# Block 0 in two halves around block 1, with raw weight words loaded into their own slots

## The chip, the cores and the metric

The kernel runs on one core of one Trainium2 chip. The metric is the device time in microseconds (us); what is quoted is the median over runs. One profiled execution gives the trace that is read here.

## The reference, cut to what matters

Attention over keys and values that are averaged by eights, then two feed-forward layers on the same 4608 tokens. All inputs are of 32 or 64 bits; the two `w` of the first layer and of the second come as 64-bit words and are decoded on the chip.

```python
# q, k, v: (8 batches, 8 heads, 576, 64); pool = 8
k_p = k.reshape(B, H, Sp, pool, D).mean(axis=3)       # v_p likewise
attn = softmax(q @ k_p^T / sqrt(D))
x = (attn @ v_p)            # -> 4608 tokens x 512

h = x @ w_in                # 512 -> 2048
y = (h * cos(h)) @ w_out    # 2048 -> 512

h2 = y @ w2_in              # 512 -> 1024
solu = h2 * softmax(h2);  ln = layernorm(solu) * g_ln
out = ln @ w2_out           # 1024 -> 512
```

## The kernel before, in words

**Blocks and steps.** The tokens are cut into 9 blocks of 512 (`j`), the 2048 columns of the first layer into 16 pieces of 128 (`f`). One step is one pair (j, f); the main loop (L828) runs through 144 of them, `steps`, block by block. A step on TensorE is `h_mm` (L519, 12 matmuls into one of two PSUM buffers `h`) and, two steps late (`SK` = 2), `y_mm` (L557, 12 matmuls that add into `y`). Between the two stands a chain of small operations on 128x512 values: `t = int(h / 2pi + 1/4)` (L527, here called k, on VectorE), `t = h - 2pi t` (L532, VectorE), a sine (L536, ScalarE), `t = t * h` (L541, VectorE, one step later; it is the last reader of that `h` buffer), the rounded half of g (L543, ScalarE) and the rest of g (L547, VectorE). The matmul of step n+2 needs the `h` buffer that L541 of step n gives back.

**Decoding.** `w_in` and `w_out` are 32 chunks of 512 KB in raw words. A chunk is loaded by SyncE into a `raw` tile and goes through `Pipe`: one call of `step` moves three chunks on by one stage. Stage s1 is two operations on ScalarE (L94, L95), s2 three on VectorE (L100, L105, L110) and one addition on GpSimd (L113), s3 one copy on ScalarE (L122) and one subtraction on GpSimd (L125), into a tile `wi` or `wo`. Five calls come ahead of the main loop, and in block 0 two in every step, threaded between the operations of the chain, until all 32 chunks are done.

**Attention.** Block j+1's attention runs inside the steps of block j, from a table of half steps (`slots`, L456): scores, exponential, `norm` (L395 to L406: sums on VectorE, products `em` and `el` on GpSimd), transposes (L416, L431) with copies by ScalarE and VectorE, products with v (`av`, L448 to L454) that end in tiles `x`. Sums over eight keys or values run on GpSimd (L194, L214).

**Order.** Each engine's instructions stand in the order in which the code calls them (`manual_schedule`); an engine that waits holds up all that is behind it in its own queue. Tiles that share a tag share that pool's buffers, and a new tile waits until the old one is no longer read. The tag `s2` has four buffers, which serve the intermediate values `dec` of the decoding and the copies `yo` by which `y_out` (L562) takes a finished block out of PSUM to DRAM (`yd`). Block 8 decodes the second layer's weights with a second `Pipe` (L837), after which 36 tiles of 128 tokens run through that layer.

Of the kernel before, what the change touches and what calls it, by code (L numbers as in the profile page):

```python
# [34 lines left out]
def fused_kernel(ctx, tc, qT_d, kT_d, vN_d, vM_d, vL_d, w_in, w_out, w2_in, w2_out, g_ln, out):  # L35
# [23 lines left out]
    wp = ctx.enter_context(tc.tile_pool(name="wp", bufs=NF))  # L59
    xp = ctx.enter_context(tc.tile_pool(name="xp", bufs=2 * NPAIR))  # L60
# [4 lines left out]
    dram = ctx.enter_context(tc.tile_pool(name="dram", bufs=NB, space=bass.MemoryType.DRAM))  # L65
# [4 lines left out]
    w_in_w, w_out_w, w2_in_w, w2_out_w = (w.bitcast(I32) for w in (w_in, w_out, w2_in, w2_out))  # L70

# [11 lines left out]
    class Chunk:  # L83
        def __init__(self, kept, tag, src, g=None, pool=wp):
            self.kept, self.tag, self.src, self.g, self.pool = kept, tag, src, g, pool
# [11 lines left out]
        def s2(self):  # L97
# [6 lines left out]
            yield  # L104
# [4 lines left out]
            yield  # L109
# [5 lines left out]
        def s3(self):  # L115
            dst = self.pool.tile([P, 2, BLK], F32R, tag=self.tag, name=self.tag)
# [11 lines left out]
    class Pipe:  # L128
# [6 lines left out]
        def fill(self, most=8):  # L135

            held = [c.raw for c in self.loaded + self.one]
            while self.todo and len(held) < most:
                c, raw = self.todo[0]
                if any(raw is r for r in held):  # L140
                    break
# [5 lines left out]
        def step(self):  # L147
            for _ in self.parts():
                pass

        def parts(self):

            last = self.two.pop(0) if self.two else None
            if self.one:
                c = self.one.pop(0)
                yield from c.s2()
                self.two.append(c)
# [26 lines left out]
    def kv_jobs(b, hf):  # L184


        def raw_tile(n):
            if (b, hf) < (1, 1):
                return wp.tile([P, n], F32, tag="wi", name="kvraw")
# [7 lines left out]
        def k_job(i):  # L197
# [5 lines left out]
            def add():  # L203
                if b == 0:
                    t = wp.tile([P, SP], F32, tag="wo", name="kp")
# [31 lines left out]
    def load_vn(b):  # L237
        t = v_t[b] = [wp.tile([P, 2, BLK], F32, tag="wi", name="vn") for _ in range(3)]
# [18 lines left out]
    def prep_vn(b, hf):  # L257
# [3 lines left out]
        w = wp.tile([P, 4 * D], F32, tag="wo", name="vw")  # L261
        u = wp.tile([P, 2, 4 * D], F32, tag="wo", name="vu")
        hi = wp.tile([P, 4 * D], F32R, tag="wo", name="vh")
# [48 lines left out]
    class Attn:  # L312
# [3 lines left out]
        def __init__(self, j):  # L316
            self.j = j
            self.t0 = j * BLK
            self.x = [None] * NPAIR
            self.sm, self.qT, self.e, self.em, self.el, self.eL, self.eT = ({} for _ in range(7))  # L320
            self.sg = list(segs(self.t0, BLK))

        def tile(self, shape, dt, tag, bufs=1):
            if self.j == 0:
                return wp.tile(shape, dt, tag="wo", name=tag)
# [114 lines left out]
        def av(self, p):  # L440
# [11 lines left out]
            x = self.x[p] = xp.tile([P, 2, BLK], F32R, tag="x", name="x")  # L452
# [513 lines left out]
```

## Time and profile before

| | before |
|---|---|
| median of 3 runs | 1416.4 us (1416.36 to 1416.98) |
| profiled execution | 1415.08 us |
| its span, first to last instruction | 1413.3 us |
| TensorE busy | 1355.3 us, 96% |
| VectorE busy | 982.1 us, 69% |
| ScalarE busy | 533.1 us, 38% |
| GpSimd busy | 404.2 us, 29% |
| mean granted TensorE clock | 0.985 |

The profiled execution is 1.8 us longer than its span and 1.3 us shorter than the median. The shares are means over stages that have different limits: a short stage ahead of the main loop, block 0 with the decoding, the blocks 1 to 7, block 8 with the second decoding, and the second layer. They have to be read stage by stage. A group of rows below names its view; "mean ns of one" is the duration of a single instruction, and for instructions that follow each other on one engine the distance from start to start is some 0.08 us shorter than the duration.

### The profile page before, as it was taken

What the parts mean: (1) busy time and instruction counts of PE and PEld (TensorE: products, weight loads), DVE (VectorE), ACT (ScalarE), POOL (GpSimd) and SP (SyncE); (2) the same over time, 40 slices, a digit from 0 to 9 for tenths busy, and PEclk for the clock granted to TensorE, in tenths of its full rate; (3) what the DMA queues carried; (4) which work ended last, traced back from release to release, by engine and by line L of the source; (5) the groups of instructions that cost most, each with busy time, mean ns of one, the idle gap of its engine ahead of it and who ended that gap; (6) DMA issues with size and microseconds to landing.
All of it is one profiled execution on the core that took longest, in us unless ns stands there. A gap on an engine that the chain in (4) does not pass through costs nothing.

```text
span 1413.3 us, 17197 instructions
## 1 busy us (share of the span) xinstructions
PE 1355.3 (96%) x6304; PEld 1116.3 (79%) x6304; DVE 982.1 (69%) x1690; ACT 533.1 (38%) x891; POOL 404.2 (29%) x517
## 2 busy tenths in 40 slices
PE   6778799999999999999999999899899999999998
PEld 5566688888888888888888888688788888888887
DVE  8999966666676666666666655897666666666664
ACT  5665633333343343333333333554222222222222
POOL 3787833322332241242131101453111111111110
PEclk9999999999999999999999999999999999999999
DMA  7424111111120220220120101430111111111100
GB/s 266 149 84 143 61 61 54 40 53 46 47 69 24 61 64 15 76 63 24 52 62 9 45 1 60 118 120 23 52 50 41 48 43 47 43 48 42 46 29 31
DMA packets 43236, 85.27 MB, mean 60 GB/s; under 512 B 4112, under 2 KB 13328, under 8 KB 43152
## 3 DMA queue, kind: packets, MB, share of 16 engines
q1 hardware_dynamic: 37824, 74.72, 16.8%
q10 hardware_dynamic: 5328, 9.44, 1.8%
q8 instruction: 50, 0.82, 0.3%
q14 instruction: 34, 0.28, 0.1%
HBM read 65.28 MB, written 18.87 MB: 60 GB/s over the span
## 4 chain that ended last, share of the span: by engine, by line
PE 82%; DVE 12%; POOL 2%; issue 2%; DMA 1%; ACT 1%; SPq 0%; POOLq 0%; ACTq 0%; DVEq 0%
PE y L557 23%; PE h L519 22%; PE o L689 5%; PE o L691 5%; PE o L690 5%; PE h L619 5%; PE h L618 5%; PE h L617 5%; PE sc L351 2%; PE lT L670 2%; DVE dec L110 2%; DVE dec L105 2%; DVE dec L100 2%; DMA kvraw<-in_kT 1%; DVE t L532 1%
## 5 line engine op out<-in xcount | busy, mean ns | idle before, releaser
L519 PE MATMUL h<-x,wi 128*128 128x512 f32 x1728 | 427.0, 397 | 22.0 <-DVE t L541 22.0
L557 PE MATMUL y<-g,wo 128*128 128x512 f32 x1728 | 425.3, 395 | 6.2 <-DVE g L547 4.5
L519 PEld LDWEIGHTS h<-x,wi 128*128 128x128 f32 x1728 | 327.1, 191 | 93.4 <-DVE t L541 26.0
L557 PEld LDWEIGHTS y<-g,wo 128*128 128x128 f32 x1728 | 322.0, 189 | 74.4 <-DVE g L547 6.7
L527 DVE TENSOR_SCALAR t<-h 128x512 int32<-128x512 f32 x144 | 99.1, 688 | 148.3 <-PE h L519 148.2
L536 ACT ACTIVATE t<-t,cst 128x512 f32<-128x512 f32 x144 | 104.3, 725 | 227.5 <-DVE t L532 223.0
L543 ACT CAST g<-t 128x512 fp32r<-128x512 f32 x144 | 89.1, 619 | 197.1 <-DVE t L541 191.1
L401 POOL TENSOR_TENSOR em<-e,sm 128x512 f32<-128x512 f32 x34 | 39.6, 1166 | 333.8 <-PE y L557 324.6
L657 POOL TENSOR_TENSOR sc<-sc,cst 128x1 f32<-128x1 f32 x36 | 19.8, 551 | 367.3 <-DVE sc L656 197.5
L194 POOL TENSOR_TENSOR kvraw<-kvraw 128x256 f32<-128x256 f32 (+3 forms) x128 | 86.7, 677 | 129.4 <-DMA kvraw<-in_vM 69.4
L689 PE MATMUL o<-wi,lh 128*128 128x512 f32 x288 | 116.0, 403 | 0.0
L691 PE MATMUL o<-wi,ll 128*128 128x512 f32 x288 | 113.0, 392 | 0.0
L690 PE MATMUL o<-wi,lh 128*128 128x512 f32 x288 | 113.0, 392 | 0.0
L547 DVE TENSOR_TENSOR g<-t,g 128x512 fp32r<-128x512 f32 x144 | 109.0, 757 | 1.8 <-ACT g L543 1.8
L672 ACT CAST lh<-lT 128x512 fp32r<-128x512 f32 x72 | 38.8, 590 | 189.3 <-PE lT L670 189.3
L626 DVE TENSOR_REDUCE sc<-h 128x1 f32<-128x1024 f32 x34 | 41.6, 1225 | 91.3 <-PE h L619 91.3
L532 DVE SCALAR_TENSOR_TENSOR t<-t,h 128x512 f32<-128x512 int32 x144 | 98.8, 686 | 4.4
L541 DVE TENSOR_TENSOR t<-t,h 128x512 f32<-128x512 f32 x144 | 97.2, 675 | 5.3 <-ACT t L536 5.0
L113 POOL TENSOR_TENSOR dec<-dec,raw 128x512 int32<-128x512 int32 x48 | 69.6, 1450 | 108.3 <-DVE dec L110 43.9
L619 PE MATMUL h<-wi,yl 128*128 128x512 f32 x216 | 84.2, 390 | 0.0
L618 PE MATMUL h<-wi,yh 128*128 128x512 f32 x216 | 84.0, 389 | 0.0
L617 PE MATMUL h<-wi,yh 128*128 128x512 f32 x216 | 84.0, 389 | 0.0
(139 smaller groups left out, 1908.8 us busy)
## 6 DMA issues: line engine op xcount, KB each, us to landing
raw<-in_w_in SPq DMA_DIRECT2D x24, 512.0 KB, 3.6
raw<-in_w_out SPq DMA_DIRECT2D x24, 512.0 KB, 3.5
kvraw<-in_kT SPq DMA_DIRECT2D x32, 288.0 KB, 2.9
qT<-in_qT SPq DMA_DIRECT2D x36, 256.0 KB, 3.3
yd<-yo ACTq DMA_DIRECT2D x36, 256.0 KB, 2.5
yr<-yd SPq DMA_DIRECT2D x18, 512.0 KB, 3.8
out<-o SPq DMA_DIRECT2D x36, 256.0 KB, 2.0
kvraw<-in_vM SPq DMA_DIRECT2D x24, 256.0 KB, 2.7
```

Of the source, the lines that this page charges most:

```text
L519: nc.tensor.matmul(ps, lhsT=w[:, a, kk, :], rhs=x[kk][:, b], start=(kk == 0 and i == 0), stop=(kk == KD - 1 and i == 2),)
L527: nc.vector.tensor_scalar(out=t.bitcast(I32), in0=ps, scalar1=1.0 / TWO_PI, scalar2=0.25, op0=ALU.mult, op1=ALU.add,)
L532: nc.vector.scalar_tensor_tensor(out=t, in0=t.bitcast(I32), scalar=-TWO_PI, in1=ps, op0=ALU.mult, op1=ALU.add)
L536: nc.scalar.activation(out=t, in_=t, func=AF.Sin, bias=halfpi)
L547: nc.vector.tensor_tensor(out=g[:, 1], in0=t, in1=g[:, 0].bitcast(F32), op=ALU.subtract)
L557: nc.tensor.matmul(o, lhsT=w[:, a, P * e:P * (e + 1)], rhs=g[:, b], start=(f == 0 and i == 0), stop=(f == NF - 1 and i == 2),)
L617: nc.tensor.matmul(ps[hh], lhsT=hi[:, kk, c], rhs=w[:, 0], start=first, stop=False)
L618: nc.tensor.matmul(ps[hh], lhsT=hi[:, kk, c], rhs=w[:, 1], start=False, stop=False)
L619: nc.tensor.matmul(ps[hh], lhsT=lo[:, kk, c], rhs=w[:, 0], start=False, stop=last)
L689: nc.tensor.matmul(ps, lhsT=hi[:, c], rhs=w[:, 0], start=(c == 0), stop=False)
L690: nc.tensor.matmul(ps, lhsT=hi[:, c], rhs=w[:, 1], start=False, stop=False)
L691: nc.tensor.matmul(ps, lhsT=lo[:, c], rhs=w[:, 0], start=False, stop=(c == NF2 - 1))
```

## The change

**Order of the steps.** The list of steps is turned: steps (0, 0) to (0, 7) first, then (1, 0) to (1, 15), then (0, 8) to (0, 15), then block 2 and the others as before. Below, step n is the n-th of the list, in either kernel. The sum `y` of block 0 is written out twice, after (0, 7) and after (0, 15), into two DRAM tiles, and GpSimd adds the two when the second layer loads them (`split_y`); the second layer takes the tokens of block 1 ahead of those of block 0 (`turn`).

**Pace of the decoding.** `Pipe.step` is no longer cut into parts. While the pipe has work, a step calls it once, and a second time in the odd ones of steps 0 to 7 and in every fourth one from step 8 on. The order of the chunks follows the order in which the steps need them.

**k on ScalarE.** While the pipe has work, k runs on ScalarE (`chain_k` with `AF.Copy`), else on VectorE as before.

**Attention.** Block 1's attention has to be ready at step 8, so its table of 32 half steps is squeezed to 14, in steps 0 to 6. Block 2's is drawn over steps 12 to 31. The sums over keys of batch 1 come ahead of the main loop, those of batch 2 in steps 8 and 9.

**Slots.** Each of the 32 weight tiles has a buffer of its own (`Slots`), and from the sixth chunk on raw words mostly are loaded into the buffer that the decoded chunk will take. Tiles `x` get two fixed sets of four buffers.

```diff
+    class Slots:
+        def __init__(self, tag, n):
+            self.tag, self.n, self.next = tag, n, 0
+        def tile(self, shape, dt, name, i=None):
+            if i is None:
+                i, self.next = self.next, (self.next + 1) % self.n
+            return wp.tile(shape, dt, tag=f"{self.tag}{i}", name=name)
+    wi, wo = Slots("wi", NF), Slots("wo", NF)
...
         def load(self, raw):
-            self.raw = raw
-            nc.sync.dma_start(out=raw.rearrange("p f w -> p (f w)"), in_=self.src)
+            self.raw = raw if raw is not None else self.home([P, BLK, 2], I32, "raw")
+            nc.sync.dma_start(out=self.raw.rearrange("p f w -> p (f w)"), in_=self.src)
...
+    steps = [(j, f) for j in range(NB) for f in range(NF)]
+    HF = NF // 2
+    steps[HF:2 * NF] = steps[NF:2 * NF] + steps[HF:NF]
+    first = {(0, 0), (0, HF)} | {(j, 0) for j in range(NB)}
+    last = {(0, HF - 1)} | {(j, NF - 1) for j in range(NB)}
...
+    def chain_k(j, f, eng):
         t = gp.tile([P, BLK], F32, tag="t", name="t")
+        g_t[j, f] = [t, None]
+        if eng is nc.scalar:
+            nc.scalar.activation(
+                out=t.bitcast(I32), in_=h_ps[j, f], func=AF.Copy, scale=1.0 / TWO_PI, bias=0.25)
+        else:
+            nc.vector.tensor_scalar(
+                out=t.bitcast(I32), in0=h_ps[j, f], scalar1=1.0 / TWO_PI, scalar2=0.25,
+                op0=ALU.mult, op1=ALU.add,
+            )
...
     def split_y(u):
-        r = yhl[u]
+        r = yhl[u][0]
+        for r2 in yhl[u][1:]:
+            nc.gpsimd.tensor_tensor(out=r, in0=r, in1=r2, op=ALU.add)
...
+        work = [[] for _ in range(2 * len(steps))]
+        for j in range(1, NB):
+            for i, fns in enumerate(at[j].slots()):
+                if j == 1:
+                    at_ = 7 * i // 16
+                elif j == 2:
+                    at_ = NF + 8 + 2 * i if i < 12 else 3 * NF + 3 * (i - 12) // 4
+                else:
+                    at_ = 2 * NF * (j - 1) + i
+                work[at_] += fns
...
-            if n < len(steps):
-                parts = pipe.parts()
-                next(parts, None)
-                chain_a(j, f, parts)
-            parts = pipe.parts()
...
+            if pipe.busy:
+                pipe.step()
+                if n > 0:
+                    chain_c(*steps[n - 1])
+                chain_k(j, f, nc.scalar)
+                for fn in work[2 * n]:
+                    fn()
+                if n % 2 if n < HF else n % 4 == 0:
+                    pipe.step()
+                chain_a(j, f)
```

Three places show what moves. The first is VectorE in a step with two chunks. Before (step 1), the three operations of each chunk stand between those of the chain:

```order
L541 TENSOR_TENSOR t<-t,h 128x512
L100 TENSOR_SCALAR dec<-dec 128x512
L527 TENSOR_SCALAR t<-h 128x512
L105 TENSOR_SCALAR dec<-dec 128x512
L532 SCALAR_TENSOR_TENSOR t<-t,h 128x512
L110 SCALAR_TENSOR_TENSOR dec<-raw_117,dec 128x512
L100 TENSOR_SCALAR dec<-dec 128x512
L547 TENSOR_TENSOR g<-t,g 128x512
```

After (step 3; L562, L568 and L556 are the former L541, L547 and L532, and L115, L119, L123 the former L100, L105, L110), they stand in two groups of three, and the last operation is the one that the sine waits for:

```order
L562 TENSOR_TENSOR t<-t,h 128x512
L115 TENSOR_SCALAR dec<-dec 128x512
L119 TENSOR_SCALAR dec<-dec 128x512
L123 SCALAR_TENSOR_TENSOR dec<-raw,dec 128x512
L568 TENSOR_TENSOR g<-t,g 128x512
L464 TENSOR_TENSOR x<-xo,x 128x512
L115 TENSOR_SCALAR dec<-dec 128x512
```

The first operation of the chain, k, has left this engine, and L556 now follows six operations of the decoding.

The second place is the first `y_out`. Before, it stands at step 18, when no chunk is being decoded; VectorE's rows there, with their waits (names of other engines' semaphores; DMAHW and a number is the landing of a DMA):

```order
L541 TENSOR_TENSOR t_1614<-t_1614,h_1598 128x512 [waits Activation_49]
L577 COPY yo_1667<-y_674 128x512 [waits PE_49,Activation_49,Pool_49]
L577 COPY yo_1673<-y_675 128x512 [waits PE_49,Activation_49,Pool_49]
L527 TENSOR_SCALAR t_1678<-h_1650 128x512 [waits DVE_49,PE_49]
L532 SCALAR_TENSOR_TENSOR t_1678<-t_1678,h_1650 128x512 [waits DVE_49]
```

After, the first `y_out` stands at step 10, in the middle of the decoding (L598 is the former L577, on VectorE; L600 the former L579, on ScalarE; DMAHW3, 5 and 6 are the landings of the three `yo` ahead):

```order
L562 TENSOR_TENSOR t_1212<-t_1212,h_1182 128x512 [waits Activation_49]
L598 COPY yo_1251<-y_700 128x512 [waits DMAHW3_49,PE_49,Activation_49]
L598 COPY yo_1257<-y_701 128x512 [waits DMAHW5_49,DVE_49,DMAHW6_49,PE_49,Activation_49]
L115 TENSOR_SCALAR dec_1208<-dec_1208 128x512
L119 TENSOR_SCALAR dec_1208<-dec_1208 128x512 [waits DVE_49]
```

Three of the four buffers of tag `s2` hold `dec` values there whose last readers come later in the code. The four `yo` tiles are all given the one buffer that is left.

The third place is TensorE at the start of block 1's products with v. Before (steps 5 to 6), a step's `y_mm` and the next step's `h_mm` stand between the transposes and the first product:

```order
L431 MATMUL eTp<-ident,em 128x128 x4
L557 MATMUL y<-g,wo 128x512 x12
L519 MATMUL h<-x,wi 128x512 x12
L448 MATMUL xo<-eT,vM_98 128x64
L449 MATMUL xo<-eT,vM_98 128x64
```

After (step 2; L441, L578, L458 are the former L431, L557, L448), they stand in one step, with a single `y_mm` between them, and the transposes follow the sums of the step before:

```order
L537 MATMUL h<-x,w 128x512 x24
L426 MATMUL eLp<-ident,el 128x128 x4
L441 MATMUL eTp<-ident,em 128x128 x4
L578 MATMUL y<-g,w 128x512 x12
L458 MATMUL xo<-eT,vM_98 128x64
L459 MATMUL xo<-eT,vM_98 128x64
```

The attention's stages have moved closer together: what lay some steps apart now lies within one or two.

## Rows read from the trace of the kernel before

**Rows 1.** The page, part 2: VectorE's busy tenths in 40 slices.

```profile
DVE  8999966666676666666666655897666666666664
```

**Rows 2.** Stretches: length, then busy us (instructions) of each engine, granted clock, DMA.

```profile
45.00:116.00 71.00, 54.07 (x221) 41.33 (x220) 70.42 (x98) 45.68 (x73) 54.94 (x43) 0.90 0.36 111
116.00:182.50 66.50, 54.14 (x229) 42.03 (x230) 62.61 (x89) 38.06 (x61) 50.32 (x46) 0.92 0.28 86
182.50:282.30 99.80, 99.46 (x474) 83.08 (x473) 64.51 (x113) 36.50 (x56) 31.28 (x56) 1.00 0.17 52
...
910.00:914.60 4.60, 4.56 (x13) 3.57 (x14) 4.49 (x7) 3.44 (x6) 2.29 (x3) 0.63 0.51 146
```

**Rows 3.** TensorE's waits, 40 to 172 us: total, times, longest.

```profile
PE h L519 <- DVE t L541: 17.5, 7, 5.0
```

**Rows 4.** Groups of VectorE's instructions, 40 to 172 us: busy, mean ns of one.

```profile
L105 DVE TENSOR_SCALAR dec<-dec 128x512 int32<-128x512 int32 x29 | 31.5, 1085 | 0.1
L110 DVE SCALAR_TENSOR_TENSOR dec<-raw,dec 128x512 int32<-128x512 int32 x30 | 29.8, 993 | 0.5
...
L372 DVE TENSOR_TENSOR e<-sc,mx 128x288 f32<-128x288 f32 x8 | 3.7, 457 | 0.3
...
L395 DVE TENSOR_REDUCE sm<-e 128x8 f32<-128x576 f32 x4 | 3.0, 740 | 0.0
```

**Rows 5.** Timeline of VectorE in block 0: start, duration, line.

```profile
44.81 0.42 DVE L100 TENSOR_SCALAR dec<-dec 128x512 f32<-128x512 f32 x1
...
112.18 1.52 DVE L105 TENSOR_SCALAR dec<-dec 128x512 int32<-128x512 int32 x1
...
115.93 0.67 DVE L541 TENSOR_TENSOR t<-t,h 128x512 f32<-128x512 f32 x1
...
117.46 0.41 DVE L105 TENSOR_SCALAR dec<-dec 128x512 int32<-128x512 int32 x1
117.80 0.67 DVE L532 SCALAR_TENSOR_TENSOR t<-t,h 128x512 f32<-128x512 int32 x1
```

**Rows 6.** Timeline of GpSimd, block 0, then block 8.

```profile
111.55 1.87 POOL L113 TENSOR_TENSOR dec<-dec,raw 128x512 int32<-128x512 int32 x1 [1.72 <-ACT t L536]
...
906.12 1.30 POOL L113 TENSOR_TENSOR dec<-dec,raw 128x512 int32<-128x512 int32 x1 [2.31 <-DVE dec L110]
```

**Rows 7.** Groups of GpSimd's instructions, 40 to 172 us.

```profile
L401 POOL TENSOR_TENSOR em<-e,sm 128x512 f32<-128x512 f32 x4 | 4.9, 1220 | 0.0
```

**Rows 8.** Timeline of VectorE in block 8: three starts of k, one step apart.

```profile
909.91 0.68 DVE L527 TENSOR_SCALAR t<-h 128x512 int32<-128x512 f32 x1
...
918.30 0.68 DVE L527 TENSOR_SCALAR t<-h 128x512 int32<-128x512 f32 x1
...
923.16 0.68 DVE L527 TENSOR_SCALAR t<-h 128x512 int32<-128x512 f32 x1
```

**Rows 9.** Timeline of VectorE: k of step 32, the first of block 2.

```profile
282.29 0.69 DVE L527 TENSOR_SCALAR t<-h 128x512 int32<-128x512 f32 x1 [0.85 <-PE h L519]
```

**Rows 10.** Timeline of ScalarE: a sine in block 0, a copy in `y_out`.

```profile
110.75 0.73 ACT L536 ACTIVATE t<-t,cst 128x512 f32<-128x512 f32 x1 [0.17 <-DVE t L532]
...
192.95 0.58 ACT L579 COPY yo<-y 128x512 f32<-128x512 f32 x1
```

**Rows 11.** Groups of ScalarE's instructions, 40 to 172 us.

```profile
L382 ACT ACT_TABLE_LOAD x2 | 2.6, 1283 | 0.0
...
L453 ACT CAST x<-xo 128x512 fp32r<-128x512 f32 x3 | 1.7, 580 | 0.0
```

**Rows 12.** Instructions on the tile `yo`, 180 to 300 us: last line of the answer.

```profile
DMA to landing us min/median/max: 2.4/2.4/2.6
```

**Rows 13.** Timeline of TensorE in block 8.

```profile
895.24 2.88 PE L519 MATMUL h<-x,wi 128*128 128x512 f32 x12
897.96 2.88 PE L557 MATMUL y<-g,wo 128*128 128x512 f32 x12
...
910.04 4.56 PE L519 MATMUL h<-x,wi 128*128 128x512 f32 x12 [2.60 <-DVE t L541]
```

More of the change, by code (lines that the diff above doesn't have):

```diff
@@ L139, in fill @@
                 c, raw = self.todo[0]
-                if any(raw is r for r in held):
+                if raw is not None and any(raw is r for r in held):
                     break
@@ L237, in load_vn @@
     def load_vn(b):
-        t = v_t[b] = [wp.tile([P, 2, BLK], F32, tag="wi", name="vn") for _ in range(3)]
+        t = v_t[b] = [wi.tile([P, 2, BLK], F32, "vn") for _ in range(3)]
         nc.sync.dma_start(out=t[0], in_=vN_d[b, 0:2].rearrange("i p c -> p i c"))
@@ L319, in __init__ @@
             self.x = [None] * NPAIR
+            self.x_tag = "x1" if j == 1 or j >= 2 and j % 2 == 0 else "x0"
             self.sm, self.qT, self.e, self.em, self.el, self.eL, self.eT = ({} for _ in range(7))
@@ L558, in y_mm @@
                     o, lhsT=w[:, a, P * e:P * (e + 1)], rhs=g[:, b],
-                    start=(f == 0 and i == 0), stop=(f == NF - 1 and i == 2),
+                    start=((j, f) in first and i == 0), stop=((j, f) in last and i == 2),
                 )
     def y_out(j, f):
-        if f < NF - 1:
+        if (j, f) not in last:
             return
@@ L714, in fused_kernel @@
     with tc.manual_schedule():
-        raws = new_raws()
+        raws = new_raws("x1")
         order = [c_in(0), c_in(1), c_in(2), c_out(0)]
-        for f in range(3, NF):
+        for f in range(3, HF):
             order += [c_in(f), c_out(f - 2)]
-        order += [c_out(NF - 2), c_out(NF - 1)]
+        order += [c_out(HF - 2), c_out(HF - 1)]
+        for f in range(HF, NF):
+            order += [c_in(f), c_out(f)]
         at.update({j: Attn(j) for j in range(NB)})
@@ L731, in fused_kernel @@
         kv_load(1, 0, *KV[0:2])
-        pool_w["m"] = wp.tile([P, 4, P], F32, tag="wi", name="pool_m")
-        pool_w["l"] = wp.tile([P, P], F32, tag="wi", name="pool_l")
-        raws += [wp.tile([P, BLK, 2], I32, tag="wi", name=f"raw{i}") for i in (4, 5)]
+        pw = wi.tile([P, 5, P], F32, "pool_w")
+        pool_w["m"], pool_w["l"] = pw[:, 0:4], pw[:, 4]
+        kv_load(1, 1, *KV[0:2])
         pipe = Pipe([])
         pipe.loaded += order[:4]
-        last = (17, 19, 31, 31, 26, 28, 30, 31)
-        idle = [4, 5, 0, 1, 2, 3]
-        use = []
-        for i in range(4, len(order)):
-            if i == 8:
-                idle[:0] = [6, 7]
-            r = next(r for r in idle if i <= last[r])
-            idle.remove(r)
-            idle.append(r)
-            use.append(r)
-        pipe.todo += [(c, raws[r]) for c, r in zip(order[4:], use) if r < 6][:4]
+        pipe.todo += [(order[4], wi.tile([P, BLK, 2], I32, "raw")), (order[5], raws[0])]
         pipe.fill()
@@ L820, in fused_kernel @@
         a0.av(3)
-        raws += [wp.tile([P, BLK, 2], I32, tag="wo", name=f"raw{i}") for i in (6, 7)]
-        pipe.todo += [(c, raws[r]) for c, r in zip(order[8:], use[4:])]
+        early = {7: raws[1], 9: raws[2], 11: raws[3]}
+        pipe.todo += [(order[i], early.get(i)) for i in range(6, len(order))]
         pipe.step()
-        steps = [(j, f) for j in range(NB) for f in range(NF)]
-        sl, pipe2 = None, None
+        add(1, 1, "k0", "k1")
+        work = [[] for _ in range(2 * len(steps))]
[8 more added lines that the diff above has]
+                work[at_] += fns
+        for i, nm in enumerate(KV[0:2]):
+            work[NF + 2 * i].append(lambda nm=nm: kv_load(2, 0, nm))
+            work[NF + 2 * i + 1].append(lambda nm=nm: add(2, 0, nm))
+        pipe2 = None
         SK = 2
@@ L871, in fused_kernel @@
             if n < len(steps):
-                if sl:
-                    for fn in sl[2 * f + 1]:
-                        fn()
+                for fn in work[2 * n + 1]:
+                    fn()
                 if pipe2 and f > 0:
```

134 lines of the change are left out of this document (60 added, 74 removed).

## The prediction

> **What bounds the kernel now.** I read VectorE's tenths first [rows 1]: 9 in slices 2 to 4 (35 to 141 us), and again near slice 25 (block 8), 6 or 7 elsewhere. The stretches say the same by stage [rows 2]. From 182.5 to 282.3 us (steps 16 to 31) TensorE is busy 99.46 of 99.8 us: sixteen steps and one block's attention at TensorE's pace. In steps 0 to 7 (45 to 116 us) it is busy 54 of 71 us, while VectorE is busy 70.4. TensorE's largest wait there is for L541, which gives back the `h` buffer: 17.5 us [rows 3]. So block 0 is set by VectorE, and the rest by TensorE. A step that TensorE sets takes two times 2.72 us (895.24 to 897.96), 5.44 us [rows 13]; sixteen are 87.0, so one block's attention costs TensorE 12.8 us.
>
> Why VectorE is full: L105 takes 1085 ns in the mean and L110 993 [rows 4], but L105 also runs in 0.41 us [rows 5]. The slow one at 112.18 started while GpSimd's L113 ran (111.55 to 113.42) and ended 0.28 us after it, the bare operation; L532, which reads PSUM, took 0.67 in block 0 [rows 5, 6]. The decoding on VectorE and GpSimd's additions exclude each other. From start to start the bare three operations of a chunk are 0.34, 0.34 and 0.6, some 1.3 us; GpSimd has two of 1.3 us [rows 6].
>
> The most that can be won is what lies above TensorE's pace between step 0 (its first decoding operation starts at 44.81) and k of step 32 (282.29) [rows 5, 9]: 237.5 less 32 x 5.44 and 2 x 12.8, 37.8 us.
>
> **The change part by part.** Slots, the order of the second layer's tokens and the loads from their new places move no work onto the path: loads are issued up to eight chunks ahead, and the two added GpSimd additions of `split_y` fall in the last stage, where GpSimd is nearly idle. I count nothing; were their cover gone, two operations of perhaps 2.6 us each, twice L113's width [rows 6].
>
> *A step's length while VectorE sets it.* Block 8 of the kernel before is the model, because its decoding stands in groups of three, as all of it will. A step with two chunks took 8.39 us (909.91 to 918.30), with one 4.86 [rows 8]. Taking k off VectorE saves 0.6 (0.68 less 0.08); on ScalarE it is a copy out of PSUM like L453's 580 ns [rows 11], bounded above by the sine's 0.73 [rows 10], and ScalarE has room for either. Against it, L532 now ends the step and L541 opens the next, with only the sine between: 0.73 us and a hand-over, 0.85, in which VectorE has nothing unless attention stands there. So 8.6 and 5.1; L547 now precedes GpSimd's addition rather than meeting its subtraction, which can give back 0.8: 7.8 and 4.3. I take 8.3 and 4.8.
>
> *Steps 0 to 7.* Four of each kind: 52.4 us. Block 1's whole attention on VectorE comes on top: eight pairs of L371 and L372 at about 0.85 [rows 4], 6.8; four sums of 0.74 [rows 4] with two small followers, 4; ten copies of about 0.6, 6.1: 17 us. Then waits that the squeezing uncovers. The exponentials of steps 1 and 4 stand behind a table load of 1.28 [rows 11] in front of the sums: 2 x 2. The transposes of steps 2 and 5 need GpSimd's products (`em` 1.22 [rows 7] and two smaller ones), queued behind a chunk's two operations: 2 x 1.5. The products with v in steps 2 and 6 stand behind a `y_mm` of 2.72, then a copy on ScalarE: 3.4 and 2.4. Together 13; attention fills the sine's gap in about six steps, 5 back. Sum 77.4, say 77, against 71.1 before (44.81 to 115.93 [rows 5]). Twelve chunk calls instead of sixteen are done by then, but all of the attention instead of half.
>
> *Steps 8 and 9.* 8.3 and 4.8.
>
> *Step 10, y_out.* The four `yo` share one buffer, so each copy waits until the one before it has landed in DRAM. VectorE, with two of the copies, stands in line, and behind it the chain and all decoding; ScalarE likewise; TensorE's `y_mm` of the new sum waits for the last copy. A link is a copy of 0.58 [rows 10] and 2.4 to landing [rows 12], 3.05 with hand-overs. From the end of L541: 0.8 (copy of g ahead on ScalarE), three links, the last copy 0.6: 10.6 us. Before, this `y_out` met no decoding. It can't be cheaper than about 10, since nothing else may run on those queues. The Trainium skill (DMA: Bandwidth & Descriptors, "Anatomy of one DMA") gives a DMA a fixed cost of about 2.0 us plus its bytes at 436 GB/s, an estimate of 2.6 us for 256 KB; by it the sum would be 0.6 us longer. The row above measures 2.4.
>
> *From there.* L541 of step 9 ends at 44.8 + 77 + 8.3 + 4.8 + 0.6 = 135.5, the last `yo` at 146.1. Then TensorE has half a `y_mm`, 1.4; 21 steps, 114.2; block 2's attention, 12.8. After an idle time of 2.6 us, the 12 matmuls at 910.04 took 4.56 us instead of 2.88 [rows 13], at a granted clock of 0.63 [rows 2], a mixture of 1.2 and 2.4 GHz: 1.7. Steps 11 to 20 on VectorE: eight single steps and two double ones, 55.0; attention (two pairs of scores 3.4, sums 2, a table load each way 3, GpSimd's value sums in the way 2), 10.4; 65.4 against TensorE's 54.4 + 3.0. The second `h` buffer lends 2.5, so TensorE loses 5.5. From step 21 on VectorE has a third of its time free. End of step 31: 146.1 + 1.4 + 114.2 + 12.8 + 1.7 + 5.5 = 281.7; `h_mm` of step 32 takes 2.72: its k starts at 284.4 instead of 282.29. **The change adds 2.1 us**: the decoding is spread and gains some 14 us on block 0, and y_out's line and the squeezed attention give it back. The profiled execution, 1415.1, would become 1417.2; the median, 1.3 above it, 1418.5.
>
> **The rivals.** *Faster: the lock alone sets the pace.* What if VectorE's order costs nothing, and only the exclusion between VectorE's decoding and GpSimd counts? Steps 0 to 7 lose four chunks at 1.3 + 2.6, 15.6 us, and gain two pairs of GpSimd's products, some 4.6: 71.1 - 11.0 = 60.1 instead of 77, so 1418.5 - 17 = 1401.5. For it: steps 0 to 7 of the kernel before are well described by that sum alone (GpSimd's 32 x 1.3, VectorE's 16 x 1.3 and 8 x 0.6, products 4.6: 71.8, key sums left out). Against it: before, decoding and chain stood interleaved and half the attention as wide apart; now there are true waits in VectorE's line. The Trainium skill (SBUF — State Buffer, "Who interferes with whom") says that the pair of ports that VectorE and GpSimd share is an exclusive lock held for the whole instruction, and that an operation reading PSUM beside one SBUF input doesn't take it. By that rule alone the time would be this rival's; the traces agree with the lock (the operation at 112.18), not yet with its being the only bound.
>
> *Slower: the squeezed attention goes round.* Scores to exponential, sums to products to transposes, transposes to v: six hand-overs in seven steps. Each crosses three engines whose queues also hold decoding, and TensorE idles long enough for 1.2 GHz, as at 910.04. If each costs 1.6 us more than I gave it, 10 us: 1428. It decides when GpSimd's `el` ends later than VectorE's L547 of the following step; then the transposes hold TensorE, its `h_mm`, and the next step. For it: GpSimd is busy 54.9 of 71 us already [rows 2]. Against it: VectorE is behind TensorE in these steps, so some of it is hidden.
>
> *It doesn't spread:* if VectorE's line stalls so long at step 10 that chunks run late for steps 16 to 23, TensorE waits for weights. Chunks are due four or more steps after their s3; I give it little, and about 1423.
>
> **How the numbers follow.** About 0.2%, 2.8 us, is what a measurement of this kernel can tell from no change. My forecast, 1418.5 within 5 either way, has chance 0.40: 0.27 of it within 0.2% of 1416.4 (up to 1419.2), 0.10 above and 0.03 below. The lock rival, anywhere from 1398 to 1413, has 0.32; the slower rival, 1424 to 1433, 0.24; late weights 0.04, slower. Faster 0.35, same 0.27, slower 0.38. The range leaves out the outer part of both: 1403 to 1429.
>
> **What would show it.** Right: VectorE idle twice for some 3 us in step 10 before `yo`, the four landings some 3 us apart, TensorE's `y` waiting for the last; steps 0 to 7 at 77 us, with steps 1, 2 and 5 the longest; steps 12 and 16 near 8.3 and their neighbours at 5.44; from step 21 TensorE full. Wrong: steps 0 to 7 near 60 us (the lock alone), VectorE idle in them less than 5 us, or waits of TensorE for the decoded `w` in steps 16 to 23.

## The result, and the profile after

| | before | after |
|---|---|---|
| median beside each other | 1416.7 us (1416.4 to 1417.9) | 1430.6 us (1428.7 to 1433.1) |
| profiled execution | 1415.08 us | 1430.76 us |
| its span | 1413.3 us | 1429.0 us |
| TensorE busy | 1355.3 us, 96% | 1358.9 us, 95% |
| VectorE busy | 982.1 us, 69% | 953.5 us, 67% |

The change makes the kernel slower by 1.0%: ratio 1.0098, 95% interval 1.008 to 1.0115. The forecast was 1418.5 us, so 12 us are missing from it, and the time lies 1.6 us above its range, close to the price of its slow rival (1428), but mostly for other reasons: the copies at `y_out` are dearer than forecast, the loop begins later, and both are shown below.

Three stretches of the trace after, by the columns of [rows 2]: steps 0 to 7 (from the first decoding operation of step 0 to L562 of step 7; L562 is the former L541), step 10 with its `y_out`, and what follows up to k of step 32.

```profile
49.14:127.98 78.84, 54.65 (x237) 44.23 (x238) 59.27 (x97) 49.85 (x78) 47.94 (x45) 0.83 0.34 129
142.62:166.48 23.86, 12.81 (x43) 9.55 (x42) 4.81 (x9) 4.84 (x8) 6.21 (x8) 0.79 0.49 177
166.48:299.45 132.97, 127.43 (x586) 104.84 (x585) 95.27 (x160) 69.12 (x112) 66.54 (x81) 0.99 0.12 39
```

VectorE was busy 70.42 of 71 us in the first stretch before [rows 2]; now it is 59.27 of 78.84. It no longer sets these steps. In step 10 it works 4.81 us of 23.86.

TensorE's waits from 49 to 180 us, beside [rows 3], and VectorE's from 49 to 142:

```profile
PE eLp L426 <- POOL el L416: 16.2, 2, 8.7
PE y L578 <- DVE yo L598: 11.1, 2, 7.7
```

```profile
DVE x L464 <- ACT x L463: 9.4, 4, 4.1
DVE sm L405 <- ACT e L392: 4.8, 2, 2.8
DVE eL L432 <- ACT eL L431: 2.8, 2, 1.5
```

The 17.5 us that TensorE waited for VectorE's L541 are gone. In their place it waits twice for GpSimd's products `el` of the squeezed attention and twice for the copies `yo`. VectorE waits for three links of the same attention. Behind the 8.7 us for `el` TensorE is slow as well: the 12 matmuls of `y_mm` (L578, at 73.75) took 4.49 us, in a stretch whose granted clock was 0.64, between the levels of 1.2 and 2.4 GHz; elsewhere they take 2.9. The groups of VectorE's decoding, 49 to 180 us (L115, L119, L123 are the former L100, L105, L110), beside [rows 4], to which the row of L100 before belongs, shown first:

```profile
L100 DVE TENSOR_SCALAR dec<-dec 128x512 f32<-128x512 f32 x29 | 21.5, 742 | 0.2 <-ACT dec L94 0.2
```

```profile
L123 DVE SCALAR_TENSOR_TENSOR dec<-raw,dec 128x512 int32<-128x512 int32 x20 | 15.3, 766 | 0.7
L115 DVE TENSOR_SCALAR dec<-dec 128x512 f32<-128x512 f32 x19 | 15.2, 798 | 0.0
L119 DVE TENSOR_SCALAR dec<-dec 128x512 int32<-128x512 int32 x19 | 14.7, 774 | 0.7
```

So a chunk's three operations cost VectorE 2.34 us instead of 2.82. L119 takes 774 ns where L105 took 1085, L123 766 where L110 took 993; L115 is a little dearer than L100. Whether the grouping or the slower pace does it (20 chunks in 131 us, 30 in 132 before) no run separates.

VectorE's timeline at the places that [rows 5] and [rows 9] show of before: the first decoding operation of step 0, step 10, and k of step 32.

```profile
49.14 0.42 DVE L115 TENSOR_SCALAR dec<-dec 128x512 f32<-128x512 f32 x1
...
142.62 0.69 DVE L562 TENSOR_TENSOR t<-t,h 128x512 f32<-128x512 f32 x1 [0.79 <-ACT t L558]
151.77 0.69 DVE L598 COPY yo<-y 128x512 f32<-128x512 f32 x1 [8.46 <-DMA yda<-yo]
158.04 0.69 DVE L598 COPY yo<-y 128x512 f32<-128x512 f32 x1 [5.58 <-DMA yda<-yo]
...
165.00 0.69 DVE L556 SCALAR_TENSOR_TENSOR t<-t,h 128x512 f32<-128x512 int32 x1 [4.15 <-ACT t L546]
...
299.45 0.69 DVE L549 TENSOR_SCALAR t<-h 128x512 int32<-128x512 f32 x1 [2.00 <-PE h L537]
```

Step 0 begins 4.3 us later than before, k of step 32 17.2 us later (282.29 to 299.45). From there the two traces run side by side: the distance is 16.8 at step 143, and the second layer takes 1.1 us of it back.

### The profile page after: what moved, and what is told of

It reads as the page before. It is cut to its first block, busy times and chain, and to the rows that moved or that the text cites. A ratio compares the mean times of both kernels' runs of the same rounds, so it can differ in the third digit from the quotient of the medians.

```text
span 1429.0 us, 17167 instructions
## 1 busy us (share of the span) xinstructions
PE 1358.9 (95%) x6304; PEld 1120.6 (78%) x6304; DVE 953.5 (67%) x1665; ACT 545.3 (38%) x914; POOL 408.7 (29%) x527
## 4 chain that ended last, share of the span: by engine, by line
PE 81%; DVE 5%; ACT 2%; issue 1%; DMA 0%; POOL 0%; ACTq 0%; POOLq 0%; DVEq 0%
PE y L578 23%; PE h L537 23%; PE o L720 5%; PE o L721 5%; PE o L722 5%; PE h L648 5%; PE h L647 5%; PE h L646 5%; PE lT L699 2%; PE sc L361 2%; PE eTp L441 1%; PE xo L460 1%; DVE dec L119 1%; DVE dec L123 1%; DVE t L556 1%
## 5 line engine op out<-in xcount | busy, mean ns | idle before, releaser
L578 PE MATMUL y<-g,w 128*128 128x512 f32 x1728 | 429.0, 397 | 16.7 <-DVE yo L598 12.7
L537 PE MATMUL h<-x,w 128*128 128x512 f32 x1728 | 425.3, 396 | 9.4 <-DVE t L562 9.4
L578 PEld LDWEIGHTS y<-g,w 128*128 128x128 f32 x1728 | 324.1, 190 | 85.8 <-DVE yo L598 14.7
L537 PEld LDWEIGHTS h<-x,w 128*128 128x128 f32 x1728 | 327.4, 191 | 80.1 <-DVE t L562 12.4
L549 DVE TENSOR_SCALAR t<-h 128x512 int32<-128x512 f32 x123 | 84.8, 689 | 137.0 <-PE h L537 136.9
L720 PE MATMUL o<-w,lh 128*128 128x512 f32 x288 | 115.8, 402 | 0.0
L721 PE MATMUL o<-w,lh 128*128 128x512 f32 x288 | 113.0, 392 | 0.0
L722 PE MATMUL o<-w,ll 128*128 128x512 f32 x288 | 112.9, 392 | 0.0
L646 PE MATMUL h<-w,yh 128*128 128x512 f32 x288 | 112.2, 390 | 0.0
L648 PE MATMUL h<-w,yl 128*128 128x512 f32 x288 | 112.2, 390 | 0.0
L647 PE MATMUL h<-w,yh 128*128 128x512 f32 x288 | 112.0, 389 | 0.0
L562 DVE TENSOR_TENSOR t<-t,h 128x512 f32<-128x512 f32 x144 | 97.5, 677 | 21.6 <-ACT t L558 21.4
L568 DVE TENSOR_TENSOR g<-t,g 128x512 fp32r<-128x512 f32 x144 | 108.5, 754 | 2.4 <-ACT g L564 2.4
L556 DVE SCALAR_TENSOR_TENSOR t<-t,h 128x512 f32<-128x512 int32 x144 | 98.7, 686 | 10.8 <-ACT t L546 6.6
```

What stands on the lines that cost most here:

```text
L537: nc.tensor.matmul(ps, lhsT=w[:, a, kk, :], rhs=x[kk][:, b], start=(kk == 0 and i == 0), stop=(kk == KD - 1 and i == 2),)
L556: nc.vector.scalar_tensor_tensor(out=t, in0=t.bitcast(I32), scalar=-TWO_PI, in1=h_ps[j, f], op0=ALU.mult, op1=ALU.add)
L562: nc.vector.tensor_tensor(out=t, in0=t, in1=h_ps.pop((j, f)), op=ALU.mult)
L568: nc.vector.tensor_tensor(out=g[:, 1], in0=t, in1=g[:, 0].bitcast(F32), op=ALU.subtract)
L578: nc.tensor.matmul(o, lhsT=w[:, a, P * e:P * (e + 1)], rhs=g[:, b], start=((j, f) in first and i == 0), stop=((j, f) in last and i == 2),)
L646: nc.tensor.matmul(ps[hh], lhsT=hi[:, kk, c], rhs=w[:, 0], start=first, stop=False)
```

## The experiments

The theories that the expectations name. **A**: the loss is the line of copies at `y_out` and the later start. **B**: the squeezed attention sets the pace and takes back whatever is gained elsewhere. Later, with the first traces in hand, **S**: the attention's hand-overs set steps 0 to 7. **V**: VectorE's own line sets them. A ratio compares a run with the kernel before on the same chip (1417.3 to 1418.0 us in these sets, 1416.7 beside the changed kernel). Where only a part moved, I compare the starts of L562 of the same step in two traces.

### The line at y_out

The four `yo` of the first `y_out` get buffers of their own:

```diff
-            if j == NB - 2:
+            if j == NB - 2 or (j, f) == (0, HF - 1):
```

> The changed kernel, but the four copies of block 0's first sum get two tiles of their own (the buffers that block 7's copies use already) instead of one shared buffer. Theory A (the line at y_out): TensorE waits 7.7 and 3.3 us there for the copies; with four buffers about 1.6 us is left, as in block 8 of the kernel before, so 9 to 10 us come back: about 1421. Rival B (the squeezed attention sets the pace, and the line at y_out is time in which the rest catches up): at most 3 us come back: 1427 or more.

Measured: 1416.1 us, ratio 0.9994 (0.9985 to 1.0003). VectorE's two copies there, the wait at the end of each row:

```profile
143.70 0.69 DVE L598 COPY yo<-y 128x512 f32<-128x512 f32 x1 [1.23 <-ACT yo L600]
145.55 0.69 DVE L598 COPY yo<-y 128x512 f32<-128x512 f32 x1 [1.16 <-ACT yo L600]
```

The waits of 8.46 and 5.58 are gone, and step 10 takes 9.7 us (L562 to L562) instead of 23.9, although the four stores land later than in the changed kernel (7.8 to 9.0 us after their issue, last section). So it is the shared buffer that makes a landing count. The line costs 14.5 us of the time, more than A gave it. B in its strict form falls: nothing takes the gain back.

### The key sums of batch 0

One line of the change, of which the text ahead doesn't speak, had moved the sums over the keys of batch 0's odd pairs from VectorE to GpSimd. Undone:

```diff
-                if b == 0 and i == 0:
+                if b == 0:
```

> The changed kernel, but all key sums of batch 0 are taken on VectorE again, as in the kernel before (the change had moved two of the four to GpSimd). Theory A: the first decoding operation of step 0, 4.3 us later in the changed kernel (49.1 against 44.8), comes back to within 1 us of 44.8, and nearly all of it reaches the end: about 1426.5. Rival B: the start is later because of the two extra loads of keys of batch 1 ahead of the raw words; then nothing comes back: 1430.

Measured: 1427.4 us, ratio 1.0067 (1.0052 to 1.0082), 3.1 us below the changed kernel by the medians, 4.4 by the ratios; in the trace L562 is 3.8 us earlier at step 0 and 4.6 at step 32. A's value holds. The start itself differs between executions: over all traces of this document L562 of step 0 begins at 52.5 to 54.4 us with the sums on VectorE (nine, the run without attention left out) and at 56.2 to 57.0 with two on GpSimd (four). The means lie 3.1 us apart, so about 1 of the 4.3 us may be chance. TensorE's waits before 49 us in the changed kernel show the place:

```profile
PE sc L361 <- POOL kT L222: 3.6, 1, 3.6
```

The scores behind it begin at 16.73 us, with the sums on VectorE at 14.15; the eight matmuls after them then take 3.62 us instead of 2.56.

### The loads ahead of the first landing

In the changed kernel SyncE stands from 94.96 to 141.46 us at the load of batch 2's second key, which waits for the one buffer `kv`; behind it the weights' loads have piled up. SyncE's issues:

```profile
94.96 0.40 SPq L104 DMA_DIRECT2D raw<-in_w_in  x1
141.46 0.33 SPq L208 DMA_DIRECT2D kvraw<-in_kT  x1
141.88 0.38 SPq L104 DMA_DIRECT2D raw<-in_w_out  x1
```

Four more of 512 KB follow up to 143.74. The tile `yo`'s DMAs in step 10, first of the changed kernel:

```profile
DMA to landing us min/median/max: 2.3/2.5/6.9
```

The 6.9 is the first of the four, issued at 144.72; by [rows 12] they took 2.4. The edit asks for the second key three steps later:

```diff
-            work[NF + 2 * i].append(lambda nm=nm: kv_load(2, 0, nm))
-            work[NF + 2 * i + 1].append(lambda nm=nm: add(2, 0, nm))
+            work[NF + 8 * i].append(lambda nm=nm: kv_load(2, 0, nm))
+            work[NF + 8 * i + 1].append(lambda nm=nm: add(2, 0, nm))
```

> The changed kernel, but the second load of batch 2's keys stands in step 12 instead of step 9. In the changed kernel it holds up SyncE's queue until 141.5 us, and then five loads of raw words go out together just ahead of the first copy of y_out, whose landing takes 6.9 us instead of 2.4. Theory A: that burst is the reason; the landing takes 2.4 to 3 us and some 4 us come back: about 1426.5. Rival B: the landing is slow because of the store itself or the ScalarE queue; it stays near 7 us, and the time at 1430.

Measured: 1429.6 us, ratio 1.0081 (1.0066 to 1.0096). Two loads of 512 KB are still issued ahead of the store (139.97 to 141.2 us), and its landing took:

```profile
DMA to landing us min/median/max: 2.3/2.5/4.2
```

So 4.2 us, not the 2.4 to 3 that A asked for. Step 10 is 2.7 us shorter. At step 32 the run is 3.0 us ahead, but 0.8 of it lie before step 0, where the two kernels are the same. The medians differ by 1.0, the ratios by 2.4 us, and the intervals overlap. The mechanism is seen; its size in the time is unsure. (By the medians the three edits are worth 14.5, 3.1 and 1.0 us alone; the third can add nothing where no copy waits for a landing.)

### The three together

> The three edits together: own tiles for the copies, key sums on VectorE, second key load late. Theory A: the line at y_out and the start are nearly all of the loss: 4 from the start, 10 to 11 from y_out (the load's 4 us lie within them): 1430.5 less 14 to 15, about 1416, the level of the kernel before, or a few us under it if the decoding then really is spread. Rival B: 1424 or more.

Measured: 1414.1 us, ratio 0.9966 (0.9954 to 0.9978). It is a few tenths of a per cent below the kernel before, and the traces of the two agree within 0.5 us from step 32 on. With line and late start gone, the changed kernel is as fast as the old one, not faster; steps 1 to 7 still take what they took after:

```profile
54.37:125.30 70.93, 50.30 (x225) 40.73 (x224) 51.96 (x86) 45.49 (x72) 40.84 (x35) 0.86 0.35 132
```

VectorE is idle for 19 us of these 70.93. The kernel before spent 64.2 us on them (L541 at 51.77 and 115.93). What follows is built on this kernel.

### The order around the sine

L556 and the sine go ahead of the step's second chunk:

```diff
+                chain_a(j, f)
                 if n % 2 if n < HF else n % 4 == 0:
                     pipe.step()
-                chain_a(j, f)
```

> The previous kernel with three edits (1414.1 us) and one more: the second operation of the chain stands ahead of the step's second chunk, so that VectorE decodes while the sine runs. Theory V (VectorE's own line sets steps 0 to 7, and the gap of 0.85 us behind the sine is paid in each step with two chunks): four such steps there and some later ones, 1414.1 less 3 to 4, 1410 to 1411. Theory S (the squeezed attention's hand-overs set these steps: in the trace of the three edits VectorE is busy 52 of 70.9 us in steps 1 to 7, TensorE waits 17.2 us for GpSimd's el, VectorE 9.9 for ScalarE's x): the gap lies beside other waits, 1413 to 1414.5.

Measured: 1413.8 us (1409.7 to 1415.9, ten runs), ratio 0.997 (0.9955 to 0.9984). Steps 1 to 7 took 70.55 us: the gap of the sine was worth next to nothing there, 0.4 us, as S says. (This trace is 2.4 us ahead at step 32; 1.9 of it lie before the loop, where the code is the same.)

### Block 1's attention left out

Every function of block 1's attention is dropped from the table, and `x` of block 0 is used again:

```diff
+            if j == 1:
+                at[1].x = a0.x
             for i, fns in enumerate(at[j].slots()):
+                if j == 1:
+                    fns = [fn for fn in fns if not fn.__defaults__]
```

> The three edits, and block 1's attention left out altogether (block 1 is fed block 0's tokens, so this part of the computation is missing). It prices the squeezed attention in steps 0 to 7. By the prediction's terms (17 us on VectorE, 13 of waits, 5 given back) steps 1 to 7 fall from 70.9 us to 4 x 8.3 + 3 x 4.8 = 47.6 us, total about 1391. Theory S, with VectorE's decoding spread and never the bound without attention: these steps come down to TensorE's 5.44 or little more in single ones and some 7 in double ones, 42 to 45 us, total 1385 to 1389.

Measured in two executions: 1390.9 us, ratio 0.9808 (0.9784 to 0.9833). Steps 1 to 7 in its trace:

```profile
50.31:99.96 49.65, 37.74 (x143) 28.16 (x144) 40.68 (x54) 32.56 (x54) 34.25 (x28) 0.94 0.53 210
```

49.65 us: the prediction's lengths give 47.6 and S 42 to 45. So without attention the steps are about as long in sum as the prediction said, and they don't fall to TensorE's pace. One by one the first takes 10.7 us, then those with two chunks 7.8 and those with one 5.1 to 5.3. VectorE is idle 9 us, 5.5 of them the seven gaps behind the sine, which were in the prediction. With what is saved ahead of step 0's L562 (54.37 to 50.31), the attention costs 25.3 us, which the prediction's terms (17 + 13 - 5) also give. The run doesn't tell VectorE's line from the lock rival: by that rival's terms the seven steps come to 11 x 3.9 + 7 x 0.6 = 47.1 us.

### The same attention by another table

Of the 25 us the waits can be tested. GpSimd's queue and TensorE's first transposes in the changed kernel:

```profile
69.51 1.22 POOL L411 TENSOR_TENSOR em<-e,sm 128x512 f32<-128x512 f32 x1
70.69 1.39 POOL L416 TENSOR_TENSOR el<-e,sm 128x128 f32<-128x128 f32 x2
```

```profile
72.14 1.11 PE L426 MATMUL eLp<-ident,el 128*128 128x128 f32 x4 [8.73 <-POOL el L416]
```

The products of a pair stand behind two operations for a chunk, and TensorE's queue, with the transposes put at once, stops until the second pair is done. The other table:

```diff
-                    at_ = 7 * i // 16
+                    at_ = {2: 0, 4: 1, 5: 1, 6: 2, 7: 3, 10: 6, 12: 7, 13: 8, 14: 3, 15: 9, 18: 4, 20: 5,
+                           21: 5, 22: 8, 23: 9, 26: 11, 28: 12, 29: 13, 30: 14, 31: 14}.get(i, 0)
```

> The three edits, and block 1's attention in the same steps 0 to 7 by another table: the second pair of heads' scores stand ahead of the first pair's transposes, and transposes and products with v come one and a half to two steps behind the sums instead of half a step. The same work, the same engines, longer from hand-over to hand-over. Theory S: the 17.2 us of TensorE's waits for el and most of VectorE's 9.9 for x go, steps 1 to 7 fall from 70.9 to 55 to 60 us, total 1399 to 1405. Theory V (VectorE's line sets the pace, waits only move): 1411 to 1415.

Measured: 1408.2 us, ratio 0.9926 (0.9906 to 0.9946). Steps 1 to 7 and what TensorE waits for in them:

```profile
53.32:118.08 64.76, 52.68 (x228) 41.55 (x228) 51.03 (x85) 43.36 (x72) 40.17 (x35) 0.87 0.37 145
```

```profile
PE sc L361 <- issue: 5.9, 1, 5.9
...
PE eLp L426 <- POOL el L416: 0.2, 1, 0.2
```

The wait for `el` fell from 17.2 to 0.2 us, but only 6.2 of these 17 came out of the steps. The rest turned into other waits: the scores' 5.9 us end at 69.22, just behind the operation of VectorE that reads the PSUM buffer which they need (it ends at 69.12; the view names no releaser), and VectorE is without a gap there from 53 to 70 us. The time lies between the two expectations: the waits do cost something, as S says, but most of them only moved, as V says. On the changed kernel itself, the table alone:

> The changed kernel with the other table of block 1's attention and nothing else. On the kernel with the three edits it gained 5.9 us (1414.1 to 1408.2). Theory A and S together (the line at y_out and the squeezed attention are separate losses, one after the other): the same here, 1424 to 1425.5. If the line at y_out takes back what the steps ahead of it gain, since GpSimd's key sums, the held loads and the landing behind them are what it waits for: 1428 to 1431.

Measured: 1424.3 us, ratio 1.0052 (1.0037 to 1.0067), 6.3 us below the changed kernel, as expected. The line at `y_out` keeps its length (step 10 takes 24.5 us). The losses are separate and add up.

### The lock between VectorE and GpSimd

On the kernel with the other table, GpSimd's addition of each chunk is cut to an eighth, and the subtraction reads the value without the low words:

```diff
-            nc.gpsimd.tensor_tensor(out=f, in0=t, in1=lw, op=ALU.add)
+            nc.gpsimd.tensor_tensor(out=f[:, 0:64], in0=t[:, 0:64], in1=lw[:, 0:64], op=ALU.add)
...
-                f = self.f.bitcast(F32)
+                f = self.t.bitcast(F32)
```

> The other table (1408.2 us), with GpSimd's addition of each chunk cut to an eighth of its width and the low words left out of the rest (that part of the computation is missing), so that GpSimd's time on decoding halves, some 1.3 us less for each chunk. VectorE's three decoding operations, now 0.76, 0.74 and 0.71 us in steps 1 to 7, should come down by about half of what they stand above 0.42, 0.43 and 0.69. Theory V with the lock as one cost among others: 3.7 us less in steps 1 to 7 and 1 to 3 elsewhere, 1402 to 1404. The lock alone as the bound (the prediction's fast rival): 1.3 us for each of 11 chunks in steps 1 to 7 and 9 in steps 8 to 20, 14 us in the first alone, 1394 or less. Theory S: 1406 to 1408.

Measured in two executions: 1390.9 us, ratio 0.9811 (0.9785 to 0.9837), 17 us below the table's. Steps 1 to 7, and VectorE's groups in them:

```profile
53.16:113.77 60.61, 50.84 (x233) 40.19 (x232) 48.06 (x85) 42.83 (x72) 29.16 (x37) 0.93 0.41 159
```

```profile
L119 DVE TENSOR_SCALAR dec<-dec 128x512 int32<-128x512 int32 x11 | 7.5, 681 | 0.4
L115 DVE TENSOR_SCALAR dec<-dec 128x512 f32<-128x512 f32 x11 | 5.7, 521 | 0.0
```

In steps 1 to 7 it is worth 4.2 us, V's value, where the lock alone would have given 14. VectorE's decoding became 3.3 us cheaper there in sum. But 7.4 us came from steps 8 to 20, where I expected 1 to 3, and another 6.6 from block 8, with the second layer's decoding. Steps 8 to 20, with the full addition and with the short one:

```profile
118.08:206.09 88.01, 82.36 (x353) 66.28 (x352) 66.81 (x103) 56.73 (x92) 60.25 (x58) 0.97 0.12 40
113.77:194.39 80.62, 77.56 (x344) 62.91 (x344) 60.66 (x104) 55.00 (x92) 42.54 (x57) 1.00 0.14 44
```

VectorE's busy time fell by 3.0 us in steps 1 to 7, by 6.2 in steps 8 to 20 and by 6.1 in block 8, each time 0.5 to 1.2 us less than the stretch gained. In block 8 the larger part is L568, an operation of the chain (1011 to 775 ns). In steps 8 to 20 TensorE's waits fell from 5.4 to 2.7 us, and its granted clock rose from 0.97 to 1.00. So in all three places the time follows what VectorE's operations cost, as V says, and only the size that I gave the later places was too small. The total came out below the 1394 of the lock alone, but that rival placed its 14 us in steps 1 to 7. The edit also lets GpSimd's subtraction start without the addition's result and frees GpSimd earlier; what that gives apart from VectorE's cheaper operations isn't separated by this run.

### Order and k, with the other table

> The other table (1408.2 us) and the chain's second operation ahead of the step's second chunk, both together. With the waits for el gone, VectorE stands in line again in steps 0 to 2 (no idle time from 43 to 70 us in the trace of the table), so the sine's gap of 0.85 us should now count where it did not before. Theory V: 3 to 5 us less, 1403 to 1405. Theory S (hand-overs still set the pace): 0 to 2 less, 1406 to 1408.

Measured: 1404.2 us, ratio 0.9903 (0.9882 to 0.9925). The order that was worth nothing with the attention's waits is worth 3.9 us without them (3.3 by the ratios), 2.9 of it in steps 1 to 7. That is V's value. This is the fastest version, 13.7 us below the kernel before in the same set.

The same with k on VectorE throughout (`chain_k(j, f, nc.vector)`):

> As the run before, and k back on VectorE in all steps. It prices the move of k to ScalarE. Theory V: 0.6 us in each step in which VectorE is the last to arrive, 8 to 14 steps among the first 20, so 5 to 8 us more than the run before. Theory S: VectorE has idle time of 13 us in steps 1 to 7 that takes it up, and one hand-over from ScalarE is saved: within 1.5 us of the run before.

Measured: 1408.3 us, ratio 0.9932 (0.9914 to 0.9951): 4.1 us dearer, between the two expectations. In steps 1 to 7 the two agree (61.4 and 61.8 us); the 5 us come from steps 8 to 20. So k on ScalarE is worth 4 us, at another place than the first steps.

### Fewer second chunks

On table and order, second chunks in steps 18 and 21 instead of 8, 12, 16 and 20:

```diff
-                if n % 2 if n < HF else n % 4 == 0:
+                if n % 2 if n < HF else n in (18, 21):
```

> The table and the order (1404.2 us), with the second chunk of a step taken in steps 18 and 21 instead of 8, 12, 16 and 20, where VectorE has less attention beside it. It tests the prediction's term of 5.5 us for VectorE being short in steps 11 to 20. By that term: TensorE loses next to nothing in these steps, 5 us less, about 1399. By the trace of the run with table and order, in which TensorE waits only 3.5 us in steps 11 to 20 and is busy in all of step 8: at most 3.5, 1401 to 1403. If the weights then come late for steps 19 to 23: TensorE waits for w, 1405 or more.

Measured: 1406.3 us, ratio 0.9926 (0.991 to 0.9943). At step 17 this run is 7.4 us ahead, with three second chunks fewer done by then; then the last chunks meet GpSimd's sums for batch 2, and TensorE waits for a weight, after which the ten matmuls take 4.00 us, which twelve do in 2.9:

```profile
209.95 4.00 PE L537 MATMUL h<-x,w 128*128 128x512 f32 x10 [2.80 <-POOL w L138]
```

The loss by late weights, which the prediction gave 0.04, needed only this. With steps 10 and 14 instead:

> The table and the order (1404.2 us), with the second chunk of a step taken in steps 10 and 14 instead of 8, 12, 16 and 20. In the run with steps 18 and 21 the last chunks met GpSimd's value sums, and TensorE waited for the decoded w in step 22; up to step 17 that run was 7.4 us ahead. Here no second chunk falls behind step 14 and the chunks are as early as there or earlier. By the prediction's term of 5.5 us for VectorE being short in steps 11 to 20: about 1399. By the 3.5 us that TensorE waited in the trace of table and order: 1401 to 1403. If two more second chunks are needed for the weights to be in time: TensorE waits for w again, 1404 to 1407.

Measured: 1406.0 us, ratio 0.9916 (0.9899 to 0.9932). No weight is late, and the run is 2.7 us ahead at step 20; in step 22 VectorE now waits in the preparation of batch 2's values, and TensorE behind it (the profiled execution, 1409.4 us, is the slowest of the four, so the wait may be untypical):

```profile
210.57 0.63 DVE L309 TENSOR_TENSOR vll<-v,vlh 128x64 fp32r<-128x64 f32 x1 [3.80 <-ACT vlh L308]
```

```profile
216.54 5.49 PE L537 MATMUL h<-x,w 128*128 128x512 f32 x12 [3.80 <-DVE t L562]
```

Neither run recovers VectorE's shortage in steps 11 to 20. Whether it can be recovered stays open.

## Why the prediction failed

**The start, and the costs counted at nothing: wrong.** The prediction let nothing onto the path ahead of step 0 ("I count nothing") and started its sum at 44.8. Step 0 begins at 49.14. The key sums of batch 0's odd pairs had moved to GpSimd, a line of the diff that I passed over: 4.3 us in the trace, 3.1 of the time when undone. TensorE, which takes its work in order, waits there for GpSimd's sum.

**A step's length while VectorE sets it: near.** 8.3 and 4.8 us give 47.6 for steps 1 to 7; without attention they took 49.65, most steps 7.8 and 5.2, and one 10.7.

**Steps 0 to 7, 77 us: right in sum (78.8), wrong in what it is made of.** I had VectorE filling them, with 13 us of waits. VectorE is idle 19.6 us, TensorE waits 16.2 us for `el`, and VectorE's own operations are cheaper than I had them: that the sum fits is partly luck. Steps 1, 2 and 5 are the longest, as forecast (11.5, 12.9 and 11.7 us). What the slow rival described ("then the transposes hold TensorE") came in steps 2 and 5. By its own condition step 5 meets it (`el` ends at 107.8, L568 at 102.9), and step 2 just misses it (72.1 against 72.6). Its price of 10 us on top did not come; another table takes 6 off.

**Steps 8 and 9, 13.1 us:** 14.6 (9.0 and 5.6).

**Step 10, y_out: the term that failed most.** 10.6 us from the end of L562 to the last copy; it took 15.3. The mechanism is the predicted one: VectorE idle before two copies, each for a landing, TensorE's `y` behind the last. The step that failed is "a link is a copy of 0.58 and 2.4 to landing": the first landing took 6.9 us, the other three about 2.5. I had priced it by a row [rows 12] of a stretch in which SyncE issued no load in the 5 us ahead of the stores, nor beside them. I did not follow SyncE's queue past the wait for `kv`, which lets five loads go 1 to 3 us before the store. Nor did I see what follows the line. ScalarE's next decoding operation waits until GpSimd has subtracted, which it could not begin before the line let VectorE's three operations through:

```profile
163.27 0.67 ACT L109 ACTIVATE dec<-raw 128x512 f32<-128x512 f32 x1 [3.51 <-POOL w L138]
```

k stands behind it on ScalarE, and VectorE waits 4.15 us more for k.

**From there, 138.3 us to k of step 32:** 140.8. VectorE's shortage in steps 11 to 20 was 5.5 in the sum; TensorE waits 5.4 us there.

The five misses (4.3, 1.8, 1.5, 4.7 and 2.5) make 14.8 of the 15.1 us by which k of step 32 came later than 284.4; 1.5 us of it are given back after. In the medians 12.1 us are missing, not 13.6: the profiled execution of before lies 1.3 us below the median that the forecast used, the one after 0.2 above its own. All five have the same sign. The first and the fourth are waits on a queue that I had not followed to its end, and edits show them; for the other three no run shows what was missing.

**The rivals.** *The lock alone* (60 us for steps 0 to 7) is out: they took 78.8, and the short addition gave 4.2 us in steps 1 to 7 where it asked for 14. Over the whole kernel the short addition is worth more than I thought, 17 us, and VectorE's operations became cheaper by as much: as far as this run shows, the lock costs by way of VectorE's line. *It doesn't spread*: TensorE waits for `w` only 3.4 us from 49 to 180; it took the run with steps 18 and 21 to bring that rival out. *The range* ended at 1429. It cut the slow rival's own bounds (1424 to 1433) short, and the forecast's terms had been given no common margin, though most of them could only be too small.

## What to carry to other kernels

When a change moves a store into a busy stage, read which loads the queues will let go just ahead of it, and price the landing from a row with that traffic in flight; a shared buffer makes each landing a link of the chain. When a table is squeezed, check each hand-over on the queue of the engine that waits: work that is ready later than it is called holds everything behind it. The waits are not the price, though: calling the same work later ended 17 us of them here and gained 6. A reordering that is worth nothing beside a larger wait may be worth its price when that wait is gone, so try it again.

## What the runs showed of the hardware that I had not expected

**Landing beside loads.** The same store of 256 KB from SBUF to DRAM landed 2.4 us after its issue with no load in flight, 4.2 us behind two loads of 512 KB (and one of 288) that went out within 3.3 us ahead of it, and 6.9 us behind five (and one). With buffers of their own, four stores in a row behind the five loads:

```profile
DMA to landing us min/median/max: 7.8/8.6/9.0
```

The Trainium skill (DMA: Bandwidth & Descriptors, "Anatomy of one DMA") gives a DMA on the path issued by GpSimd a fixed part of about 2.0 us and its bytes at 436 GB/s; here SyncE and ScalarE issue. Taken over the six loads and the store together, 3.2 MB, that is an estimate of 9.3 us from the first load's issue at 141.46, so 150.8; the store landed at 151.6. For the run with the second key late (three loads and the store, 1.6 MB, from 139.97) the same estimate gives 145.7; the store landed at 147.4. Read as a queue of bytes, the page's rule for one DMA falls 0.8 and 1.7 us short here.

**What GpSimd's additions cost on VectorE.** Cutting GpSimd's addition from 1.45 to 0.46 us (means in steps 1 to 7) for 48 chunks, 32 at the start and 16 in block 8, took 17 us off the kernel. VectorE's busy time over the profiled execution fell by as much, from 956.5 to 938.9 us, 2.3 us of it ahead of the loop. A chunk's three operations became 0.3 us cheaper in steps 1 to 7 and 0.4 in steps 8 to 20; in block 8 L568, which belongs to no chunk, gained more than they did. Pricing the addition by the decoding's operations in one stage alone gave too little.
